# Shared slots for weights times values, transposes in 64-row tiles, and dummy matmuls at the start

## The chip, the cores and the metric

One core of one Trainium2 chip runs the kernel. The metric is the device time of one execution in microseconds; the median of three runs before is 609.94 us (609.64 to 611.61). The engines named are TensorE (PE; its weight loads stand apart as PEld), VectorE (DVE), ScalarE (ACT), GpSimd (POOL) and SyncE (SP, which issues most of the DMAs). Each works through its own queue in order; they wait for each other by semaphores.

## The reference

Attention with a threshold, then a gated feed-forward layer. Batch 8, 8 heads, sequence 576, head size 64; 4608 tokens of 512 go into the second part, whose hidden width is 1536.

```python
scores = scale * np.matmul(q, k.transpose(0, 1, 3, 2))
thresh = np.max(scores, axis=-1, keepdims=True) - tau
scores = np.where(scores >= thresh, scores, -1000000000.0)
attn = np.exp(scores - np.max(scores, axis=-1, keepdims=True))
attn = attn / (np.sum(attn, axis=-1, keepdims=True) + 1e-09)
x = np.matmul(attn, v)                    # heads side by side: 4608 x 512
xn = x / np.sqrt(np.mean(x * x, axis=-1, keepdims=True) + 1e-06) * rms_g
g = xn @ w_gate
out = (g * (1.0 / (1.0 + np.exp(-g))) * (xn @ w_val)) @ w_out
```

## The kernel before

**Tiling.** Queries go in chunks of 128: four "main" chunks for each batch (512 of the 576 rows), and for each two batches one "joined" chunk of their two tails of 64 rows. That makes 36 chunks. Heads go in pairs, four to a chunk, since the 64 channels of two heads fill 128 partitions. A chunk with a pair of heads is a step; there are 144, numbered s.

**A step.** `emit_s` issues the score burst, in float32: for either head (a half of the rows of the array) 512 columns and 64 tail columns, into `s_ps` (two tiles of two banks). These are matmuls of 64 rows; in a joined chunk they are 64 rows by 64 columns. VectorE passes over the scores of each head (line 441), which copies them to `ssb` and takes the maximum. GpSimd makes the threshold (448), ScalarE masks and exponentiates, or GpSimd masks (459 to 497). The weights `wsb` are transposed to `wt`: on TensorE in the first 16 steps (508 to 522), by DMA afterwards (525). `emit_av` multiplies with the values (544; in a joined chunk 549), ten matmuls of 128 rows (in a joined chunk twenty), into `ot`, one bank that two steps fill by halves. After every second step `emit_half` divides by the sums (570, 571), and the next matmuls into `ot` wait for it. After the fourth pair, `emit_x` normalizes the chunk and transposes it by DMA.

**The feed-forward part** (`emit_ffn`) works on groups of one to four chunks: for each of 12 blocks of the hidden width four matmuls for the gate (633) and four for the value (638), tanh on ScalarE (647), two passes on VectorE (650, 655); then 12 matmuls a chunk for the output (674).

**Inputs.** For each batch and pair `emit_qk` loads k and q (128 rows of 4 x 128) and transposes them on TensorE: four full 128 by 128 transposes for k, four for q (273), each four in a bank of their own, which VectorE or ScalarE copies to `qkT` (281, 283). The tails of k are transposed in 64-row tiles (304), those of q in full ones (321).

**Banks.** PSUM has eight banks: four for `s_ps`, one for `ot`, three in `ring`. From the ring come the banks of the feed-forward products, of all transposes of q and k, and of the first steps' transposed weights. After the last scores the four banks of `s_ps` join it.

**The order** is worked out in Python before the launch. Each piece of work is an `Op` with an engine, an estimated cost, a priority (mostly the step at which it is due), its dependencies, and how many ring banks it takes. `order_ops` plays the program through: of what an engine could do next it takes what can start first, and among equals what is due first. The instructions are issued to each engine in that order. A "gated" Op also depends on the score burst of a given step, so that a load isn't issued too early.

**Start.** The identity and constants are made, the first q and k are loaded, and TensorE starts with their transposes. The feed-forward weights are loaded and cast to float16 during the first steps (725 to 729). The cast of the gate weights is planned on VectorE and that of the value weights on GpSimd; the function that issues it reads `w_dram` when it is called, after the loop, so both are issued on GpSimd.

Of the kernel before, what the change touches and what calls it, by code (L numbers as in the profile page):

```python
# [15 lines left out]
COST = dict(  # L16
    s_main=1260.0, s_virt=1250.0, tr4=480.0, tr8=560.0, av_main=360.0, av_virt=500.0, ffn4=216.0,
    ttr=690.0, evac_qk=600.0, evac_kt=350.0, prelu=700.0, exp2=1250.0, exp1=690.0, exp0=690.0,
    mask_d=750.0, mask_g=1740.0, take_g=1300.0,
    trw=560.0, evac_w=420.0, rz=180.0, xmul=400.0, sq=800.0, xn=750.0, pool_tiny=270.0, pool_mean=800.0, pool_dma=800.0, cast_v=720.0, cast_vt=380.0, cast_w=720.0, sp=350.0, sp_tr=1300.0, sp_qk=1310.0, sp_tl=630.0,  # L20
)


class Op:
    __slots__ = ("eng", "cost", "prio", "deps", "fn", "ring", "frees", "slot", "end", "start", "dma", "opens", "nring")

    def __init__(self, eng, cost, prio, deps, fn, ring=None, frees=None, dma=0.0, nring=1):
# [5 lines left out]
        self.nring = nring  # L33


def order_ops(ops, ring_sizes):
# [17 lines left out]
    dma_free = 0.0  # L54
    out = []
    ready_at = {i: 0.0 for i in range(len(ops))}
    while len(out) < len(ops):
        best = None
        for e, lst in pending.items():
# [4 lines left out]
            for i in lst:  # L64
# [6 lines left out]
                k = (t, o.prio, i)  # L71
# [5 lines left out]
        o = ops[i]  # L77
        o.start = t
# [6 lines left out]
        eng_free[e] = t + o.cost  # L85
        if o.dma:
            dma_free = max(dma_free, t + 300.0) + o.dma
            o.end = max(dma_free, t + o.cost) + (1400.0 if o.cost == COST["sp_tr"] else 2000.0)
        else:
            o.end = t + o.cost  # L90
# [17 lines left out]
def kernel(  # L108
# [120 lines left out]
    def setup():  # L229
        o_id = add("POOL", 2000.0, -100, [], lambda o: make_identity(nc, id32))  # L230

        def consts(o):
            nc.vector.memset(zrow, 0.0)
# [9 lines left out]
        o_c = add("DVE", 400.0, -100, [o_id], consts)  # L243
# [8 lines left out]
    def emit_qk(b, p, prio):  # L252
# [16 lines left out]
        done = []  # L269
        for j in (1, 0):  # L270
            def tr(o, j=j):
                for c in range(4):
                    nc.tensor.transpose(ring[o.slot[0]][:, 128 * c:128 * c + 128],  # L273
                                        nat[:, j, c].rearrange("s h d -> s (h d)"), id32)

            t = add("PE", COST["tr4"], prio, [los[1 - j], o_id] + last_s.get(("k", b - 2, p), []), tr, ring="R")
# [550 lines left out]
```

## Time and profile before

| what | value |
|---|---|
| median of three runs | 609.94 us (609.64 to 611.61) |
| the profiled execution | 609.41 us |
| its span, first to last instruction | 607.3 us |
| mean granted TensorE clock | 0.999 |
| ScalarE: prelu pass (459), 224 times | 766 ns |
| weights transposed by DMA (525) | 128 times, median 3.0 us to landing |

The page gives each engine's busy time as a union of its instructions. TensorE's matmuls overlap, so their lengths are longer than the distance from one to the next; a group's true price on TensorE is read from its first start to the start of what follows. In a row of the timeline stand the start and the length of a run of equal instructions, the line, the shape and the count; "64*128" is the part of the array used, rows by columns. In a row of stretches stand its bounds and length, busy time and count of PE, PEld, DVE, ACT and POOL, then the clock, the DMA engines' busy share and GB/s.

### The profile page before, as it was taken

Reading aid. Unit: us, or ns where it says so; the run is one execution under the profiler, and the core shown is the slowest. Engines: PE = TensorE matmul, PEld = TensorE weight load, DVE = VectorE, ACT = ScalarE, POOL = GpSimd, SP = SyncE. Lnnn points to the kernel's source line nnn. Section 1 sums busy time; section 2 is a strip of 40 time slices with the busy share of each in tenths; the row PEclk is TensorE's granted clock in tenths of the full one; section 3 lists DMA queues with packets and bytes.
Section 4 is the critical chain, followed back from the end, with each engine's and each line's share of the span. In section 5 each row is a group of like instructions: output and inputs, shape, how many; then the busy total and the mean of one; then the engine's idle time right before and its main releaser. Section 6 shows DMA issues by size and latency. Waiting matters only on the chain.

```text
span 607.3 us, 13784 instructions
## 1 busy us (share of the span) xinstructions
PE 583.5 (96%) x5008; PEld 351.4 (58%) x5008; DVE 428.4 (71%) x1105; ACT 464.0 (76%) x741; POOL 322.2 (53%) x462
## 2 busy tenths in 40 slices
PE   5899899999999999999999999999999999999995
PEld 4676566767676555555555455555545445555663
DVE  3888775969686687748874887388747784887453
ACT  3898786878788888868886888688868886887332
POOL 0457774646475765654664557455565554653000
PEclk9999999999999999999999999999999999999999
DMA  9999797786786478677777467966779555435210
GB/s 180 251 238 225 146 166 180 161 159 122 181 166 157 108 146 165 157 179 131 173 167 167 103 132 175 189 140 148 141 177 168 105 89 126 119 87 101 65 37 35
DMA packets 271123, 88.99 MB, mean 147 GB/s; under 512 B 253648, under 2 KB 263376, under 8 KB 271056
## 3 DMA queue, kind: packets, MB, share of 16 engines
q1 hardware_dynamic: 268400, 86.28, 65.5%
q0 software_dynamic: 1600, 1.57, 1.7%
q8 instruction: 39, 0.64, 0.5%
q10 hardware_dynamic: 1056, 0.26, 0.2%
q14 instruction: 28, 0.23, 0.1%
HBM read 37.75 MB, written 9.44 MB: 78 GB/s over the span
## 4 chain that ended last, share of the span: by engine, by line
PE 69%; DMA 7%; issue 6%; ACT 6%; POOL 5%; DVE 5%; SPq 1%; DVEq 0%; POOLq 0%; ACTq 0%
PE s_ps L408 19%; PE ring L633 11%; PE ring L674 11%; PE ring L638 11%; DMA wt<-wsb 6%; PE ot L544 5%; PE ring L273 3%; PE s_ps L420 2%; ACT ssb L459 2%; DVE ssb L441 2%; POOL wsb L497 2%; POOL wsb L492 1%; PE s_ps L633 1%; DVE sl L650 1%; PE s_ps L638 1%
## 5 line engine op out<-in xcount | busy, mean ns | idle before, releaser
L441 DVE CUSTOM_DVE_ANT_0 ssb<-s_ps,zrow 128x576 f32<-128x576 f32 x288 | 208.8, 753 | 72.1 <-PE s_ps L408 62.2
L459 ACT ACTIVATE ssb<-ssb,nth 128x576 f32<-128x576 f32 x224 | 165.2, 766 | 39.4 <-POOL nth L448 38.9
L408 PE MATMUL s_ps<-qkT 64*128 64x512 f32 x512 | 156.6, 645 | 1.8 <-DVE mx L441 1.0
L448 POOL TENSOR_SCALAR nth<-mx 128x2 f32<-128x2 f32 x144 | 31.6, 220 | 158.3 <-DVE mx L441 147.3
L492 POOL TENSOR_SCALAR wsb<-ssb,nth 128x576 f16<-128x576 f32 x64 | 110.5, 1726 | 5.9
L638 PE MATMUL ring<-xnT,wv 128*128 128x512 f16 (+2 forms) x536 | 109.7, 327 | 1.4 <-DVE sl L650 1.2
L633 PE MATMUL ring<-xnT,wg 128*128 128x512 f16 (+2 forms) x536 | 109.3, 326 | 0.7 <-DVE wt L519 0.5
L466 ACT ACTIVATE wsb<-ssb 128x1152 f16<-128x1152 f32 x80 | 92.9, 1162 | 2.2
L674 PE MATMUL ring<-wo,hf 128*128 128x512 f16 x408 | 93.1, 379 | 0.0
L408 PEld LDWEIGHTS s_ps<-kTt,qkT 64*128 64x128 f32 x512 | 57.9, 188 | 55.8 <-issue 53.2
L650 DVE SCALAR_TENSOR_TENSOR sl<-th,ring 128x512 f32<-128x512 f32 (+2 forms) x134 | 73.5, 548 | 22.3 <-ACT th L647 21.6
L647 ACT ACTIVATE th<-ring 128x512 f32<-128x512 f32 (+2 forms) x134 | 64.2, 482 | 32.2 <-PE ring L633 31.5
L497 POOL TENSOR_TENSOR wsb<-wsb,esb 128x576 f16<-128x576 f16 x64 | 81.7, 1277 | 6.2 <-ACT esb L478 1.7
L655 DVE TENSOR_TENSOR hf<-ring,sl 128x512 f16<-128x512 f32 (+2 forms) x134 | 74.6, 557 | 8.6 <-PE s_ps L408 0.5
L633 PEld LDWEIGHTS <-wg 128*128 128x128 f16 x624 | 54.2, 98 | 33.3 <-issue 3.5
L638 PEld LDWEIGHTS <-wv 128*128 128x128 f16 x624 | 53.5, 98 | 32.6 <-issue 2.4
L674 PEld LDWEIGHTS <-hf 128*128 128x128 f16 x432 | 40.4, 98 | 46.5 <-issue 1.7
L544 PEld LDWEIGHTS <-wt 128*128 128x128 f16 x1280 | 52.2, 97 | 21.5 <-DMA wt<-wsb 7.5
L544 PE MATMUL ot<-va,wt 128*128 128x65 f16 x1280 | 60.0, 194 | 3.5 <-DMA wt<-wsb 3.3
L408 PEld LDWEIGHTS s_ps<-qkT 64*128 64x128 f32 x512 | 45.1, 185 | 30.7 <-issue 13.1
L478 ACT ACTIVATE esb<-ssb,nth 128x576 f16<-128x576 f32 x64 | 49.3, 770 | 10.6 <-POOL nth L448 10.3
L408 PE MATMUL s_ps<-kTt,qkT 64*128 64x64 f32 x512 | 49.9, 245 | 0.0
(54 smaller groups left out, 521.3 us busy)
## 6 DMA issues: line engine op xcount, KB each, us to landing
qkn<-in_k_dram SPq DMA_DIRECT2D x64, 128.0 KB, 3.1
vst<-in_v_dram SPq DMA_DIRECT2D x32, 256.0 KB, 3.2
out_dram<-osb SPq DMA_DIRECT2D x32, 256.0 KB, 2.7
qkn<-in_q_dram SPq DMA_DIRECT2D x62, 128.0 KB, 3.0
stage<-in_moe_w_gate_dram SPq DMA_DIRECT2D x12, 256.0 KB, 3.8
stage<-in_moe_w_val_dram SPq DMA_DIRECT2D x12, 256.0 KB, 4.0
wt<-wsb SPq DMA_TRANSPOSE x128, 3.0
wo<-in_moe_w_out_dram POOLq DMA_DIRECT2D x4, 384.0 KB, 8.0
```

The costliest lines, as they stand in the source:

```text
L408: nc.tensor.matmul(s_ps[h][:, at[h]:at[h] + n], qkT[b % 2][p][hs, c], src[hs], start=True, stop=True)
L441: nc.vector.tensor_tensor_reduce(out=ssb[a][:, h], in0=s_ps[h][:, ROW_AT[h]:ROW_AT[h] + S], in1=zrow, scale=-1.0 / 8.0, scalar=3.0e38, op0 ...
L459: nc.scalar.activation(out=ssb[a][:, h], in_=ssb[a][:, h], func=PRELU, scale=-1.0, bias=nth[m][:, h:h + 1], **PRELU_KW)
L466: nc.scalar.activation(out=wsb[s % NW], in_=ssb[a], func=AF.Exp)
L492: nc.gpsimd.tensor_scalar(out=wsb[s % NW][:, h], in0=ssb[a][:, h], scalar1=nth[m][:, h:h + 1], scalar2=None, op0=ALU.is_le)
L497: nc.gpsimd.tensor_tensor(out=wsb[s % NW][:, h], in0=wsb[s % NW][:, h], in1=esb[es], op=ALU.mult)
L544: nc.tensor.matmul(ot[:, cs], w[:, 4 * h + j], va[b % 2][:, p, V_AT[h][j]], start=(j == 0), stop=(j == 4))
L633: nc.tensor.matmul(ring[o.slot[0]][:, 0:n], wg[d][:, fs], xnT[slot][:, d, 0:n], start=(d == 0), stop=(d == 3))
L638: nc.tensor.matmul(ring[o.slot[0]][:, 0:n], wv[d][:, fs], xnT[slot][:, d, 0:n], start=(d == 0), stop=(d == 3))
L650: nc.vector.scalar_tensor_tensor(out=sl[i][:, 0:n], in0=th[i][:, 0:n], scalar=1.0, in1=ring[g.slot[0]][:, 0:n], op0=ALU.add, op1=ALU.mult)
L655: nc.vector.tensor_tensor(out=hf[hi][:, 0:n], in0=ring[vv.slot[0]][:, 0:n], in1=sl[i][:, 0:n], op=ALU.mult)
L674: nc.tensor.matmul(ring[o.slot[0]], hf[hs[fc][0]][:, 128 * j:128 * (j + 1)], wo[:, fc], start=(fc == 0), stop=(fc == NFC - 1))
```

## The change

1. **q and k in 64-row tiles.** From batch 1 on (`ROW_FROM`), `emit_qk` makes one Op of the transposes of k and q: sixteen transposes of 64 rows, alternating between the upper and the lower half of the rows, the upper into one ring bank and the lower into another. It takes both banks at once, waits for both loads, is gated by the score burst at its step, and has the priority -500, so that it comes first of what can start when that burst ends. The copies split by row half and write runs of 64 columns. The k tails get the same gate and priority; the q tails become eight 64-row transposes in two banks with two copies on ScalarE.
2. **Weights times values.** `ot` is gone; the ring has four banks. `emit_av` is called after every second step and issues both steps' matmuls (20, in a joined chunk 40) into one bank of the ring; reciprocal and product follow on VectorE as before and free the bank.
3. **Dummy matmuls.** `zrow` is cleared first, and eight matmuls of 512 columns of zeros into `s_ps` are the first work of TensorE.
4. **The order.** Estimated costs are new, and each Op of TensorE has a mode (full, 64-row, and the two of the joined chunks). A change of mode costs `SWITCH` = 170 ns in the plan. `BIAS`, which would let work of the same mode go first, is 0.
5. **Gate weights.** Their cast is planned on GpSimd, too.

`emit_s` is written in another way and issues the same matmuls in the same order; `N_ALT` equals `N_PE` and changes nothing.

```diff
+SWITCH = 170.0
...
-                k = (t, o.prio, i)
+                other = e == "PE" and o.mode != mode
+                k = (t + (BIAS if other else 0.0), o.prio, i)
...
+        cost = o.cost
+        if e == "PE":
+            if o.mode != mode:
+                t -= BIAS
+                cost += SWITCH
+            mode = o.mode
...
-    ot = ps("ot", 512)
-    ring = [ps(f"ring{i}", 512) for i in range(3)]
+    ring = [ps(f"ring{i}", 512) for i in range(4)]
...
+    HALF = (slice(0, 64), slice(64, 128))
...
+        o_z = add("DVE", 350.0, -200, [], lambda o: nc.vector.memset(zrow, 0.0))
+
+        def warm(o):
+
+            for _ in range(8):
+                nc.tensor.matmul(s_ps[0][:, 0:512], zrow[:, 0:128], zrow[:, 0:512], start=True, stop=True)
+
+        o_w = add("PE", COST["warm"], -200, [o_z], warm)
...
+        if b >= ROW_FROM:
+            def tr(o):
+                for j in (1, 0):
+                    for c in range(4):
+                        for r, rs in enumerate(HALF):
+                            at = 256 * j + 64 * c
+                            nc.tensor.transpose(ring[o.slot[r]][:, at:at + 64],
+                                                nat[rs, j, c].rearrange("s h d -> s (h d)"), id32[rs, rs])
+
+
+            t = gated(add("PE", COST["tr_qk"], -500.0, los + [o_id] + last_s.get(("k", b - 2, p), []), tr, ring="R",
+                          nring=2, mode=1), prio)
...
+                        nc.scalar.copy(out=dst[:, :, rs], in_=src)
...
+                        nc.vector.tensor_copy(out=dst[:, :, rs], in_=src)
...
-        t = add("PE", COST["tr4"], prio, [tail_load["k", b], o_id] + deps, tr, ring="R")
+        t = add("PE", COST["tr4"], prio if b < ROW_FROM else -500.0, [tail_load["k", b], o_id] + deps, tr, ring="R", mode=1)
+        if b >= ROW_FROM:
+            gated(t, prio)
...
             for p in range(NP):
-                nc.tensor.transpose(
-                    ring[o.slot[0]][:, 128 * p:128 * (p + 1)],
-                    qtl[i % 2][:, 2 * p:2 * p + 2].rearrange("s h d -> s (h d)"), id32)
+                for r, rs in enumerate(HALF):
+                    nc.tensor.transpose(
+                        ring[o.slot[r]][:, 64 * p:64 * (p + 1)],
+                        qtl[i % 2][rs, 2 * p:2 * p + 2].rearrange("s h d -> s (h d)"), id32[rs, rs])
...
+            for i in range(2):
+                w, p = wt[(s - 1 + i) % NWT], p1 - 1 + i
+                for h in range(2):
+                    at = (2 * i + h) * (D + 1)
+                    rows = [(slice(0, 128), b % 2)] if kind == "m" else [(HALF[e], e) for e in range(2)]
+                    for rs, vi in rows:
                         for j in range(5):
-                            nc.tensor.matmul(ot[64 * e:64 * e + 64, cs], w[:, 4 * h + j, 64 * e:64 * e + 64],
-                                             va[e][:, p, V_AT[h][j]], start=(j == 0), stop=(j == 4))
+                            nc.tensor.matmul(ring[o.slot[0]][rs, at:at + D + 1], w[:, 4 * h + j, rs],
+                                             va[vi][:, p, V_AT[h][j]], start=(j == 0), stop=(j == 4))
...
-        if s >= 2:
-            deps.append(half_ev[s // 2 - 1])
-        o = add("PE", COST["av_main" if kind == "m" else "av_virt"], s + 2.5, deps, fn)
+        deps = w_ready[s - 1] + w_ready[s] + [x for bb in bs for i in range(2) for x in v_ready[bb, p1 - i]]
+        o = add("PE", 2 * COST["av_main" if kind == "m" else "av_virt"], s + AV_PRIO, deps, fn, ring="R",
+                mode=0 if kind == "m" else 3)
...
-                    eng = nc.vector if w_dram is moe_w_gate else nc.gpsimd
-                    eng.tensor_scalar(
+                    nc.gpsimd.tensor_scalar(
...
-        emit_av(s)
         if p % 2:
-            emit_half(s)
+            emit_av(s)
...
-    seq = order_ops(ops, {"R": 3})
+    seq = order_ops(ops, {"R": 4})
```

More of the change, by code (lines that the diff above doesn't have):

```diff
@@ L89, in order_ops @@
         else:
-            o.end = t + o.cost
+            o.end = t + cost
         if o.frees is not None:
@@ L570, in fn, with half @@
+        o = add("PE", 2 * COST["av_main" if kind == "m" else "av_virt"], s + AV_PRIO, deps, fn, ring="R",
+                mode=0 if kind == "m" else 3)
+        for i in range(2):
+            av_of[s - i] = [o]
+            for bb in bs:
+                last_av[bb, p1 - i] = last_av.get((bb, p1 - i), []) + [o]
+        r = rz[len(half_ev) % 3]
+        def half(_):
+            o3 = ring[o.slot[0]][:, 0:4 * (D + 1)].rearrange("p (h d) -> p h d", d=D + 1)
             nc.vector.reciprocal(out=r, in_=o3[:, :, D])
@@ L733 @@
                 lo = gated(add("SP", COST["sp"], pr, w_use[slot][-1:], load, dma=1050.0), pr)
-                ca = (add("DVE", 420.0, pr, [lo, o_g], cast) if w_dram is moe_w_gate
-                      else add("POOL", COST["cast_w"], pr, [lo, o_g], cast))
+                ca = add("POOL", COST["cast_w"], pr, [lo, o_g], cast)
                 w_use[slot].append(ca)
@@ L781 @@
 ON_ACT = 1
+BIAS = 0.0
+ROW_FROM = 1
+AV_PRIO = 2.5
+HALF_PRIO = 1.2
 WAYS = ("pg", "pp")
```

130 lines of the change are left out of this document (59 added, 71 removed).

## The prediction

> **What bounds the kernel now.** I read the head of the page first, then the busy time by stretch, then the chain that ended last.
>
> ```profile
> span 607.3 us, 13784 instructions
> PE 583.5 (96%) x5008; PEld 351.4 (58%) x5008; DVE 428.4 (71%) x1105; ACT 464.0 (76%) x741; POOL 322.2 (53%) x462
> 30.00:60.00 30.00, 29.71 (x300) 21.51 (x297) 25.71 (x73) 27.66 (x40) 20.13 (x39) 1.00 0.98 231
> 60.00:90.00 30.00, 27.56 (x318) 18.09 (x315) 23.14 (x67) 23.55 (x40) 22.14 (x30) 1.00 0.89 157
> 90.00:570.00 480.00, 474.55 (x3934) 274.31 (x3934) 343.07 (x856) 383.39 (x604) 272.52 (x373) 1.00 0.68 145
> PE 69%; DMA 7%; issue 6%; ACT 6%; POOL 5%; DVE 5%; SPq 1%; DVEq 0%; POOLq 0%; ACTq 0%
> ```
>
> From 90 to 570 us TensorE is busy 474.55 of 480 us, while ScalarE has 383, VectorE 343 and GpSimd 273. The DMA engines stand at 0.68. There, a microsecond of TensorE work saved is close to a microsecond of time. From 30 to 60 us ScalarE (27.66 of 30) and VectorE (25.71) are as full as TensorE, so I count nothing for TensorE work saved before 90 us. The chain agrees: 69% of it is TensorE.
>
> A busy TensorE is not one at its best rate, so I take costs from start to start in the timeline of TensorE. (Its columns: start, length, instruction, shape, count.)
>
> ```profile
> 150.63 1.13 PE L408 MATMUL s_ps<-qkT 64*128 64x512 f32 x4
> 151.60 0.33 PE L408 MATMUL s_ps<-kTt,qkT 64*128 64x64 f32 x4
> 151.86 0.61 PE L638 MATMUL ring<-xnT,wv 128*128 128x256 f16 x4
> ...
> 153.19 0.47 PE L544 MATMUL ot<-va,wt 128*128 128x65 f16 x10
> 153.49 0.63 PE L273 MATMUL ring<-id,qkn 128*128 128x128 f32 x4
> 153.96 0.47 PE L544 MATMUL ot<-va,wt 128*128 128x65 f16 x10
> 154.36 1.13 PE L408 MATMUL s_ps<-qkT 64*128 64x512 f32 x4
> ```
>
> A score burst holds TensorE 1.23 us (150.63 to 151.86). Ten weights-times-values matmuls take 0.30 us when a transpose follows (153.19 to 153.49) but 0.40 when a score burst follows (153.96 to 154.36). So entering the 64-row form costs 0.10 us. Leaving it: from the four small score matmuls at 151.60, two a half, to the next form are 0.26 us; two steps of 0.06 (as of the tails' transposes below, which are of the same form) are work, so some 0.15 us is the way out. Transposes and weights-times-values, both 128 by 128, follow each other without such a price.
>
> **Part 1: q and k transposed in 64-row tiles.** The old price of a batch and head pair is two groups of four 128-row transposes.
>
> ```profile
> 34.06 0.66 PE L273 MATMUL ring<-id,qkn 128*128 128x128 f32 x4
> 34.55 0.47 PE L544 MATMUL ot<-va,wt 128*128 128x65 f16 x10
> ...
> 92.07 1.07 PE L273 MATMUL ring<-id,qkn 128*128 128x128 f32 x8
> 92.97 1.89 PE L674 MATMUL ring<-wo,hf 128*128 128x512 f16 x8
> ...
> 90.00:570.00 480.00, 28.41 (x192) 21.26 (x192) 1.00 0.68 145
> ```
>
> Four cost 0.47 to 0.49 us, eight in a row 0.90. I take 0.92 for a pair of head's q and k. The last row is line 273 alone: 192 transposes between 90 and 570 us, that is 24 pairs. The other eight pairs lie before 90 us; four of them (batch 0) aren't changed anyway.
>
> The new form is 16 transposes, alternating between the two halves of the rows, into two banks. The trace has none of these, but it has the tail's transposes, which already are 64-row tiles of one half:
>
> ```profile
> 162.06 0.69 PE L408 MATMUL s_ps<-qkT 64*128 64x512 f32 x1
> 162.16 0.35 PE L304 MATMUL ring<-id,ktl 64*128 64x64 f32 x3
> L304 PE MATMUL ring<-id,ktl x4: 222/223/272, 162.0 to 162.3; 64*128 64x64 f32 x4
> ```
>
> Three span 0.35 us and one lasts 0.223, so each starts 0.06 us after the one before. They run while a score matmul of the other row half streams (162.06 to 162.75): the two halves go side by side. So 16 transposes in two halves are eight steps of 0.062, 0.50 us, if both halves are fed; one after the other they would be 1.0 us. These are my two ends, and I take 0.50, because the rows above show the halves running at once. Behind a score burst they pay no entry, and the way out only moves behind them. Saved: 0.92 - 0.50 = 0.42 us, times 24 = **10.1 us**. Where other work slips between burst and transposes, 0.10 + 0.15 comes on top. For that, two of four banks must be free at the burst's end; during its 1.23 us nothing takes a bank, so I let one in seven miss: 24/7 x 0.25 = **-0.9 us**.
>
> ```profile
> L304 PEld LDWEIGHTS ring<-id,ktl x4: 136/138/139, 162.0 to 162.2; 64*128 64x128 f32 x4
> L273 PEld LDWEIGHTS ring<-id,qkn x192: 137/141/145, 92.0 to 462.3; 128*128 128x128 f32 x192
> ```
>
> A weight load of 64 rows takes 138 ns, one of 128 rows 141. [...]
>
> The tails follow the same way.
>
> ```profile
> 429.57 0.46 PE L304 MATMUL ring<-id,ktl 64*128 64x64 f32 x4
> 429.96 1.04 PE L633 MATMUL ring<-xnT,wg 128*128 128x512 f16 x4
> 90.00:570.00 480.00, 2.75 (x24) 1.93 (x24) 1.00 0.68 145
> ...
> 490.41 0.57 PE L549 MATMUL ot<-va,wt 128*64 128x65 f16 x20
> 490.90 1.10 PE L420 MATMUL s_ps<-qkT,qTv 64*64 64x512 f32 x8
> ```
>
> A k tail between other forms costs 0.39 us plus 0.10 entry; behind a burst 4 x 0.06 = 0.24: 0.25 saved. Of the six after 90 us (24 instructions, third row, line 304 alone) the one at 162 us already sat at a burst, so 5 x 0.25 = **1.3 us**. The q tails, four full transposes at 0.49 as above, become four double steps of 0.25: three after 90 us, **0.7 us**.
>
> ScalarE and VectorE copy the same 512 columns per pair as before, in another order; each q tail becomes two ScalarE copies, off the path. The transposes now wait for both the k and the q load, which are issued three of the 144 steps (3 x 607/144 = 12.6 us) ahead.
>
> **Part 2: two pairs' weights-times-values together.** Twenty matmuls instead of ten are the same work. In the chunks of joined tails they are a form of their own (128*64): the burst at 490.41 takes 0.49 us and entry and exit are in each. Twelve of the sixteen lie after 90 us and become six: 6 x 0.2 = **1.2 us**. The waits:
>
> ```profile
> PE ot L544 <- DMA wt<-wsb: 3.3, 6, 0.9
> PEld L544 <- DMA wt<-wsb: 7.5, 11, 1.4
> ```
>
> TensorE stood between 3.3 us (matmuls) and 7.5 us (weight loads) for late transposed weights. One wait for two pairs lets the earlier of them be late for free; nothing to all of it could go, and I take **2 us**. What waits behind it in TensorE's queue is everything, which is why a late pair would now cost the same but be met half as often. The bank of `ot` joins the ring: three banks become four, and one is held per two steps. New waits for banks in an order that is worked out afresh are not in the trace; between -3 and +4 us, I take **-1.5 us**.
>
> **Part 3: dummy matmuls.**
>
> ```profile
> L273 PE MATMUL ring<-id,qkn x8: 421/421/446, 5.9 to 7.5; 128*128 128x128 f32 x8
> L273 PE MATMUL ring<-id,qkn x192: 272/273/330, 92.1 to 462.4; 128*128 128x128 f32 x192
> 5.94 1.94 PE L273 MATMUL ring<-id,qkn 128*128 128x128 f32 x8 [5.94 <-DMA qkn<-in_k_dram]
> 8.75 2.08 PE L408 MATMUL s_ps<-qkT 64*128 64x512 f32 x4 [0.26 <-DVE qkT L283]
> 11.09 2.12 PE L273 MATMUL ring<-id,qkn 128*128 128x128 f32 x12
> ```
>
> The clock column doesn't show it, but the durations do: the first transposes last 421 ns against 273 later, and the first score burst (8.75 to 11.09) takes 2.34 us against 1.23. The array starts at about half speed until some 12 us. Eight dummies of 512 columns, 0.43 us each at that speed, fill about 1.4 to 4.9 us, when TensorE waits for the first load anyway. If the clock then stays up, the first transposes and scores shrink by 0.9 + 1.1 us; if it doesn't, nothing. From 30 us on ScalarE is nearly full, and its work would start as much earlier. I take **1.5 us** of 0 to 2.
>
> That the clock falls back during the transposes from 5.94 us, so that the 1.5 us are 0, I give 0.3; the first score burst was still slow right after two microseconds of transposes. [...]
>
> **Part 4: gate weights.** The diff moves their cast from VectorE to GpSimd, but it was there:
>
> ```profile
> L729 POOL TENSOR_SCALAR wg<-stage,rmsg 128x512 f16<-128x512 f32 x12 | 8.3, 694 | 0.6
> ```
>
> The old lambda read a loop variable late. Only the order changes, before 90 us: 0.
>
> **Sum.** 10.1 - 0.9 + 1.3 + 0.7 + 1.2 + 2 - 1.5 + 1.5 = 14.4 us. The profiled execution took 609.41 us, 2.1 over its span, and lies 0.5 below the median of 609.94; span 592.9, time 595.0 against its own, 595.5 against the median: I say **595**.
>
> **The rivals.**
>
> A, *transposes away from the bursts.* If the banks are usually taken at a burst's end, other work goes first and every pair pays entry and exit: 24 x 0.25 = 6 us less than Part 1 counts, of which 0.9 is deducted already: 600. Against it: nothing takes a bank during a burst. Chance 0.12.
>
> B, *the halves do not run side by side.* Then 16 x 0.062 = 1.0 us replaces 0.92, Part 1's main term is -2 instead of 10.1, and the time is 607. For it: no row shows two transposes at once. Against it: the score matmul at 162.06 beside the tail's transposes. Chance 0.08. [...]
>
> C, *banks starve TensorE: slower.* The price comes from what holds the banks.
>
> ```profile
> L441 DVE CUSTOM_DVE_ANT_0 ssb<-s_ps,zrow 128x576 f32<-128x576 f32 x288 | 208.8, 753 | 72.1 <-PE s_ps L408 62.2
> L283 DVE COPY qkT<-ring 128x512 f32<-128x512 f32 x32 | 22.0, 688 | 22.5 <-PE ring L273 19.3 <-ACT ssb L459 2.8 <-ACT osb L680 0.3
> L647 ACT ACTIVATE th<-ring 128x512 f32<-128x512 f32 (+2 forms) x134 | 64.2, 482 | 32.2 <-PE ring L633 31.5
> L650 DVE SCALAR_TENSOR_TENSOR sl<-th,ring 128x512 f32<-128x512 f32 (+2 forms) x134 | 73.5, 548 | 22.3 <-ACT th L647 21.6
> ```
>
> Right behind a burst VectorE has two score passes (753 ns each) ahead of its copy (688): one bank is held 2.2 us from the burst's end, ScalarE's half up to 1.5 us, and a pair's weights-times-values may hold a third. The feed-forward then has one bank, and after each product must wait for 482 + 548 ns of reading, 1.0 us of idle TensorE per pair of head. It decides from 14.4 / 24 = 0.6 us per pair; at 1.0 the time is 609.4 - 14.4 + 24 = 619. Against it: at 92.07 eight transposes took two of three banks, and TensorE went on at 92.97, in the 0.90 us that eight at 0.11 need. Chance 0.06.
>
> **How the numbers follow.** Forecast 0.72, A 0.12, B 0.08, C 0.06, and 0.02 for no effect at all. D, *the clock falls back* (0.3, whatever the other case), moves a time by 1.5 us: 596.5 in the forecast, inside its bounds. The forecast's own bounds: everything in Part 1 behind bursts (+0.9), the wait term up to 5 more, banks +5 to -2, clock -1.5 to +0.5; together, not all at once, 588.5 to 601. A lies inside; reaching out toward B, the range is 588.5 to 603.5 and leaves out B, C and the rest, 0.16. A measurement here can tell about 0.3%, 1.8 us: forecast, A and most of B are faster (0.91), 0.03 the same, 0.06 slower.
>
> **What would show it.** Line 273's successor in 64*128 form, 16 matmuls spanning about 0.5 us plus a tail, directly behind line 408's rows: right; 1.0 us: B. Feed-forward or weights-times-values between them: A. TensorE idle on `sl` or `hf` beside them, more than in the page above: C. The first transposes at 273 ns: Part 3 right; 421: wrong. TensorE's idle for `wt` under 3 us: Part 2 right. Wrong in any case if, from 90 to 570 us, the busy time falls but the stretch does not shorten.

## The result, and the profile after

The changed kernel takes 595.03 us (median of four runs, 593.09 to 597.22), the kernel before on the same chip 610.29 (609.64 to 611.61). The ratio is 0.9748 with the interval 0.9703 to 0.9793: faster by 2.5%. The profiled execution of after took 597.22 us with a span of 595.1; the profiled one of before took 609.41 with 607.3.

The head of the page of after, its chain by engine, and then its view of stretches (bounds and length; busy time and count of PE, PEld, DVE, ACT, POOL; clock; DMA share; GB/s):

```profile
span 595.1 us, 14293 instructions
PE 577.8 (97%) x5256; PEld 344.3 (58%) x5256; DVE 424.9 (71%) x1105; ACT 462.9 (78%) x745; POOL 322.4 (54%) x462
PE 80%; DVE 6%; DMA 5%; ACT 4%; POOL 3%; issue 2%; SPq 1%; DVEq 0%; POOLq 0%
90.00:570.00 480.00, 475.02 (x4209) 273.22 (x4210) 347.41 (x873) 383.37 (x616) 271.38 (x369) 1.00 0.70 145
```

TensorE is still the bound, and its share of the chain rose from 69 to 80%. In the 480 us it stays as busy as before but issues 4209 matmuls instead of 3934; 176 of these 275 come of the transposes of q and k alone, which are smaller and more (368 instead of 192). So a busy share can't tell what was gained; the steps can. VectorE passes over each step's scores twice (line 483 of after); the start of the first of these passes marks the step. The table is worked out from these starts, one profiled execution each:

| us | before | after |
|---|---|---|
| start to step 48 | 186.1 | 186.7 |
| step 48 to step 143 | 366.7 | 354.7 |
| step 143 to the end | 54.5 | 53.7 |

Nearly all of the gain of these two executions, 12.0 of 12.2 us, lies in the middle. (The profiled execution of after is the slowest of its four; the medians differ by 15.3 us.)

The timeline of after, TensorE alone, at the places that were named beforehand:

```profile
94.30 0.71 PE L293 MATMUL ring<-id,qkn 64*128 64x64 f32 x16
94.94 0.61 PE L668 MATMUL ring<-xnT,wg 128*128 128x256 f16 x4
...
320.73 1.13 PE L463 MATMUL s_ps<-qkT 64*128 64x512 f32 x4
...
321.86 0.67 PE L293 MATMUL ring<-id,qkn 64*128 64x64 f32 x16
322.46 2.76 PE L709 MATMUL ring<-wo,hf 128*128 128x512 f16 x12
...
427.03 1.13 PE L463 MATMUL s_ps<-qkT 64*128 64x512 f32 x4
...
428.16 0.41 PE L345 MATMUL ring<-id,ktl 64*128 64x64 f32 x4
428.50 1.04 PE L673 MATMUL ring<-xnT,wv 128*128 128x512 f16 x4
```

A burst with sixteen transposes behind it holds TensorE 1.73 us (320.73 to 322.46), 0.50 more than the 1.23 of a burst alone; one with a k tail 1.47 (427.03 to 428.50), 0.24 more. Of the 28 pairs of head changed, 24 stand right behind a burst, 21 of the 23 after 90 us; the one at 94.30 stands alone and holds 0.64 (94.30 to 94.94) beside its entry.

TensorE's waits over the whole span, two rows of before (the bursts of main and of joined chunks stand in two lines there, in one line of after) and then, in the second fence, three of after (in all, times, the longest):

```profile
PEld s_ps L408 <- DVE mx L441: 9.5, 21, 1.2
...
PEld s_ps L420 <- DVE mx L441: 3.9, 10, 0.6
```

```profile
PEld s_ps L463 <- DVE mx L483: 25.0, 63, 1.0
PEld L589 <- DMA wt<-wsb: 2.0, 4, 0.9
PE ring L589 <- DMA wt<-wsb: 1.5, 3, 0.8
```

The waits for late transposed weights went from 3.3 us (matmuls) and 7.5 (weight loads) to 1.5 and 2.0. Another wait grew beside them: the weight loads of score bursts come up to VectorE, which still reads the scores before (`mx`), 63 times and for 25.0 us instead of 31 times and 13.4 us. A weight load that waits doesn't stop the matmuls that still run: the matmuls themselves waited 4.1 us for `mx` in after, 1.8 in before.

### The profile page after: what moved, and what is told of

The parts are those of the page before. It is cut to its first block, busy times and chain, and to the rows that moved or that the text cites. A ratio compares the mean times of both kernels' runs of the same rounds, so it can differ in the third digit from the quotient of the medians.

```text
span 595.1 us, 14293 instructions
## 1 busy us (share of the span) xinstructions
PE 577.8 (97%) x5256; PEld 344.3 (58%) x5256; DVE 424.9 (71%) x1105; ACT 462.9 (78%) x745; POOL 322.4 (54%) x462
## 4 chain that ended last, share of the span: by engine, by line
PE 80%; DVE 6%; DMA 5%; ACT 4%; POOL 3%; issue 2%; SPq 1%; DVEq 0%; POOLq 0%
PE s_ps L463 28%; PE ring L709 13%; PE ring L668 13%; PE ring L673 12%; PE ring L589 6%; DVE ssb L483 3%; DMA wt<-wsb 3%; PE ring L293 2%; ACT ssb L501 2%; PE s_ps L709 1%; PE s_ps L673 1%; PE ring L553 1%; PE s_ps L668 1%; DMA qkn<-in_q_dram 1%; ACT wsb L508 1%
## 5 line engine op out<-in xcount | busy, mean ns | idle before, releaser
L463 PE MATMUL s_ps<-qkT 64*128 64x512 f32 x512 | 162.9, 645 | 4.7 <-DVE mx L483 3.2
L668 PE MATMUL ring<-xnT,wg 128*128 128x512 f16 (+2 forms) x548 | 111.0, 325 | 0.4 <-DVE xsb L606 0.3
L463 PEld LDWEIGHTS s_ps<-kTt,qkT 64*128 64x128 f32 x512 | 61.0, 188 | 54.0 <-issue 51.3
L709 PE MATMUL ring<-wo,hf 128*128 128x512 f16 x396 | 89.9, 379 | 0.0
L463 PEld LDWEIGHTS s_ps<-qkT 64*128 64x128 f32 x512 | 48.9, 185 | 45.8 <-DVE mx L483 21.9
L673 PEld LDWEIGHTS <-wv 128*128 128x128 f16 x624 | 55.4, 98 | 34.2 <-issue 1.6
L668 PEld LDWEIGHTS <-wg 128*128 128x128 f16 x624 | 52.5, 98 | 30.9 <-issue 1.0
L589 PEld LDWEIGHTS <-wt 128*128 128x128 f16 (+1 forms) x1600 | 52.2, 100 | 12.4 <-issue 2.3
L589 PE MATMUL ring<-va,wt 128*128 128x65 f16 (+1 forms) x1560 | 56.4, 194 | 1.7 <-DMA wt<-wsb 1.5
L463 PE MATMUL s_ps<-kTt,qkT 64*128 64x64 f32 x512 | 54.3, 245 | 0.0
```

The source lines that it names most:

```text
L463: nc.tensor.matmul(s_ps[h][rows, at[h]:at[h] + n], lhs(hs), src[hs], start=True, stop=True)
L589: nc.tensor.matmul(ring[o.slot[0]][rs, at:at + D + 1], w[:, 4 * h + j, rs], va[vi][:, p, V_AT[h][j]], start=(j == 0), stop=(j == 4))
L668: nc.tensor.matmul(ring[o.slot[0]][:, 0:n], wg[d][:, fs], xnT[slot][:, d, 0:n], start=(d == 0), stop=(d == 3))
L673: nc.tensor.matmul(ring[o.slot[0]][:, 0:n], wv[d][:, fs], xnT[slot][:, d, 0:n], start=(d == 0), stop=(d == 3))
L709: nc.tensor.matmul(ring[o.slot[0]], hf[hs[fc][0]][:, 128 * j:128 * (j + 1)], wo[:, fc], start=(fc == 0), stop=(fc == NFC - 1))
```

## The experiments

The kernels differ from after as their diffs show; e9 differs from before. Each runs beside before on its chip, and only the ratios are compared from one chip to another. The order is worked out anew for every edit that changes an Op, so a difference holds the edit and its order together. Two kernels keep the order exactly: e4 is after itself, and e8 changes the order inside one Op alone.

**After again (e4).** No edit; the mark against which the others stand.

> The changed kernel once more, on the same chip as its parts: 595 us by its four runs (593.1 to 597.2). It gives the spread that the others are held against; if the dummies release the clock in some executions, the times fall into two groups about 2 us apart.

Measured: 598.39 us, ratio 0.9772 (0.9741 to 0.9803); span 593.7. Steps 48 to 143 took 353.1 us against 354.7 in the first profile of after: a difference under 2 us between two single profiles says nothing. The five times lie in two groups, 595.6 to 595.9 and 598.4 to 598.8, as expected for dummies that release the clock in some executions. But the profiled one is of the lower group, and its clock rose only at 13.27 us; so the dummies don't explain its group, and what does is open.

**Full transposes for q and k (e1).**

```diff
-ROW_FROM = 1
+ROW_FROM = 8
```

> The changed kernel with q and k of all batches transposed in full 128-row tiles again (the tails stay in 64-row tiles). If the transposes are what pays, as the prediction has it (10.1 - 0.9 us), this takes 9 us more than the changed kernel, some 604 us, and line 314 has 256 full transposes with nothing of line 293. If the new order and the fourth bank pay instead, it stays within 2 us of the changed kernel, some 596.

Measured: 603.67 us, 0.9877 (0.9841 to 0.9912), span 601.1. The 64-row form is worth 5.3 us by the medians, where Part 1 counted 9.2 for these pairs. What else the change does gains 7.8 us without it (611.5 before on this chip). e1's row of the weight loads that wait for `mx`, over the whole span, is nearly that of after:

```profile
PEld s_ps L463 <- DVE mx L483: 23.7, 59, 1.1
```

**The transposes half by half (e8).** The same sixteen, all of the upper row half first. Nothing else moves.

```diff
-                for j in (1, 0):
-                    for c in range(4):
-                        for r, rs in enumerate(HALF):
+                for r, rs in enumerate(HALF):
+                    for j in (1, 0):
+                        for c in range(4):
```

> The changed kernel with the sixteen transposes in another order: all eight of the upper row half, then all eight of the lower. If the halves run side by side only because neighbours in the queue alternate, the sixteen take 1.0 us instead of 0.5 and the time rises by 24 x 0.5 = 12 us, to 610. If each half has a queue of its own, the burst stays at 0.5 us and the time within 2 us of the changed kernel.

Measured: 597.7 us, 0.9792 (0.9765 to 0.982), span 596.1. The timeline of e8 at the same burst as above, and the stretch 90 to 570 us of the transposes alone (PE, PEld) of e8:

```profile
321.88 1.13 PE L463 MATMUL s_ps<-qkT 64*128 64x512 f32 x4
...
323.01 0.96 PE L293 MATMUL ring<-id,qkn 64*128 64x64 f32 x16
323.91 1.25 PE L709 MATMUL ring<-wo,hf 128*128 128x512 f16 x5
...
90.00:570.00 480.00, 22.93 (x371) 21.90 (x369) 1.00 0.72 145
```

The transposes now hold 0.90 us (323.01 to 323.91) where after has 0.60 (321.86 to 322.46), and are busy 22.93 us between 90 and 570 us (16.98 in after). So the halves do run side by side, and less so in e8's order than in the alternating one. And the price came out far below what such a microsecond should cost. In distances from one start to the next, summed over the span, the transposes took 25.2 us instead of 19.6, 5.6 more; score bursts took 171.1 instead of 173.3. So 2.2 of the 5.6 came back, and all of it in the 32 bursts that follow the transposes of a pair (44.6 us instead of 46.8, in e4 also 46.8; the other bursts differ by 0.1 at most). I read this as a burst that starts later and finds VectorE done; the waits don't show it, for e8's weight loads of bursts stand for `mx` 63 times and 24.9 us, as in after. Weights times values fell as well, from 44.5 to 42.9, but in e4, the same kernel as after, they took 42.7. Both kernels are, within their intervals, equally fast.

This also bears on e1. There q and k take 34.7 us of TensorE in this sum, in e8 33.3 and in after 27.4, the first four pairs included. These four took 6.5 us in e1, where the clock had risen in time, and 8.1 in e8, so for the other 28 pairs it is 28.2 against 25.2. Yet e8 is faster than e1 by 0.85% of before, 5 us. So part of what the 64-row form gains over e1 isn't TensorE's time in the transposes; its place behind a burst and the order around it are what is left, and no run separates these.

**One pair's weights times values at a time, in a bank of its own (e2).** This undoes Part 2: `ot` is back, the ring has three banks.

```diff
-    ring = [ps(f"ring{i}", 512) for i in range(4)]
+    ot = ps("ot", 512)
+    ring = [ps(f"ring{i}", 512) for i in range(3)]
...
-        if p % 2:
-            emit_av(s)
+        emit_av(s)
+        if p % 2:
+            emit_half(s)
...
-    seq = order_ops(ops, {"R": 4})
+    seq = order_ops(ops, {"R": 3})
```

> The changed kernel with the weights times values of one pair at a time in their own bank, and three ring banks, as before. By the prediction (1.2 + 2 - 1.5 us) it takes 1 to 3 us more than the changed kernel, 597. If the shared slot and the fourth bank are the real gain, 6 us more or above, over 601. If the row transposes starve on three banks, more than that, with TensorE idle for sl and hf.

Measured: 618.43 us, 1.0111 (1.0072 to 1.015), span 616.1: 20 us behind e4 and slower than before. e2's waits of TensorE over the whole span, and of the stretch 372 to 448 us one of GpSimd; then its timeline (TensorE, and one row of SyncE's queue):

```profile
PE ot L587 <- DMA wt<-wsb: 7.2, 9, 2.1
PEld L587 <- DMA wt<-wsb: 12.9, 13, 2.2
...
POOL nth L491 <- DVE mx L484: 26.5, 7, 14.4
```

```profile
420.56 1.30 SPq L283 DMA_DIRECT2D qkn<-in_q_dram  x2
...
422.04 1.45 PE L464 MATMUL s_ps<-qkT 64*128 64x512 f32 x4
...
437.32 1.03 PE L682 MATMUL ring<-xnT,wv 128*128 128x512 f16 x4
438.28 0.27 PE L294 MATMUL ring<-id,qkn 64*128 64x64 f32 x1
438.89 0.71 PE L294 MATMUL ring<-id,qkn 64*128 64x64 f32 x15 [0.34 <-DVE sl L694]
439.69 2.75 PE L718 MATMUL ring<-wo,hf 128*128 128x512 f16 x12
442.37 1.13 PE L464 MATMUL s_ps<-qkT 64*128 64x512 f32 x4
```

Two losses can be seen. Late weights cost 7.2 and 12.9 us, as in before and more. And there is one hole: no score burst starts between 422.04 and 442.37, and GpSimd waits 14.4 us for a maximum. TensorE is mostly busy there, with feed-forward work. The next burst needs q and k, whose loads were issued at 420.56 and earlier and land 3.3 us later (the median of this stretch); their transposes stand at 438.28, behind the whole feed-forward group, and wait there for a bank that the feed-forward part held (`sl`). `order_ops` shows why such an Op comes late:

```python
if len(ring_free[o.ring]) < o.nring:
    continue
t = max(t, sorted(ring_free[o.ring])[o.nring - 1][0])
```

An Op for two banks is no candidate, or a late one, while the feed-forward part takes each single bank as it comes free; its priority of -500 decides only between equal starts. This reading is of the rows and the code; an order that keeps banks back for such an Op wasn't tried.

**Neither (e5).** e2 with `ROW_FROM = 8`; dummies, tails and estimated costs stay as in after.

> The changed kernel with both undone: full transposes for q and k, and one pair's weights times values at a time in its own bank with three ring banks; new costs, tails in 64-row tiles and dummies stay. If the two parts simply add up (5 us for the transposes, 20 for the shared slot, as the first four runs gave them one by one), it takes 623 us. If instead the 64-row transposes need the fourth bank, so that the loss of the second run is theirs, it is near the kernel before: 608 to 612.

Measured: 617.97 us, 1.0145 (1.0122 to 1.0168), span 614.9. That should have been near before and is 1.5% slower. The steps place it: 367.3 us from step 48 to 143, as before (366.7), but step 16, the first joined chunk, starts at 73.7 us instead of 63.2. The timeline of e5 there:

```profile
49.39 0.66 SPq L336 DMA_DIRECT2D qtl<-in_q_dram  x1
...
62.86 1.01 PE L682 MATMUL ring<-xnT,wv 128*128 128x256 f16 x4 [1.95 <-DVE sl L694]
...
70.61 0.27 PE L366 MATMUL ring<-id,qtl 64*128 64x64 f32 x1
71.17 0.46 PE L366 MATMUL ring<-id,qtl 64*128 64x64 f32 x7 [0.29 <-DVE sl L694]
...
72.35 1.10 PE L464 MATMUL s_ps<-qkT,qTv 64*64 64x512 f32 x8
```

It looks like the same hole: the q tail, issued at 49.39 and landed 8.4 us later, is transposed only at 70.61; in its new form it, too, asks for two of three banks. That form needn't open a hole, though: in e2 and e6, with the same form and as many banks, this tail is transposed at 60.46 and 61.86. The clock fell there as well, for 3.4 us from 62.28 on, in TensorE's wait of 1.95 us (60.91 to 62.86).

**Two pairs together, but in a bank of their own (e6).** Ring of three.

```diff
-nc.tensor.matmul(ring[o.slot[0]][rs, at:at + D + 1], w[:, 4 * h + j, rs],
+nc.tensor.matmul(ot[rs, at:at + D + 1], w[:, 4 * h + j, rs],
...
-    seq = order_ops(ops, {"R": 4})
+    seq = order_ops(ops, {"R": 3})
```

> The changed kernel, two pairs' weights times values still issued together, but into a bank of their own, with three ring banks. If the missing fourth bank is what cost 20 us in the second run, this is as slow, 615 us or more, with TensorE waiting for sl, hf and mx. If issuing two pairs together is what pays, it stays within 3 us of the changed kernel, 598 to 601.

Measured: 605.69 us, 0.9927 (0.9904 to 0.9949), span 604.4. Against after's steps it loses 6.0 us in the middle (360.7) and 3.5 at the end (57.2). The waits for late weights stay away, the fourth bank is what is missing (with one bank, each two pairs also wait until VectorE has read the two before); e6's row of TensorE's waits for them, over the whole span:

```profile
PE ot L590 <- DMA wt<-wsb: 1.2, 3, 0.8
```

**A shared slot, but each pair as soon as its weights are there (e7).** Ring of four; the first pair takes the slot, the second fills it.

```diff
+            slot = (first or o).slot[0]
...
-        deps = w_ready[s - 1] + w_ready[s] + [x for bb in bs for i in range(2) for x in v_ready[bb, p1 - i]]
+        deps = w_ready[s] + [x for bb in bs for x in v_ready[bb, p]] + [first]
...
+                ring=None if p % 2 else "R", mode=0 if kind == "m" else 3)
```

> The changed kernel with four ring banks, two pairs sharing a slot, but the first pair's matmuls issued as soon as its weights are there, not together with the second's. If the fourth bank pays, it stays within 2 us of the changed kernel, 598 to 600. If waiting once for two pairs pays, it is near the second run, over 610, with TensorE idle for wt as there (6.6 us) or more.

Measured: 615.34 us, 1.0084 (1.0055 to 1.0113), span 613.6. Here the bank is there and the pairing is missing. e7's waits, and a row of its timeline ahead of step 16:

```profile
PE ring L590 <- DMA wt<-wsb: 3.3, 8, 0.8
PEld L590 <- DMA wt<-wsb: 8.0, 13, 1.1
...
65.57 1.01 PE L676 MATMUL ring<-xnT,wv 128*128 128x256 f16 x4 [3.08 <-DVE sl L688]
```

The waits for weights are back at the size of before (3.3 and 8.0 us). The slot is also held for longer, from the first pair to after the second, and the hole ahead of the first joined chunk is back as well (step 16 at 72.6 us). From step 48 to 143 it took 366.0 us.

**The 64-row pairs alone, in the kernel before (e9).** Only q and k; tails, three banks, `ot` and costs as before.

```diff
+        if b >= ROW_FROM:
...
+            t = gated(add("PE", COST["tr_qk"], -500.0, los + [o_id] + last_s.get(("k", b - 2, p), []), tr, ring="R",
+                          nring=2), prio)
...
+ROW_FROM = 1
```

> The kernel before with nothing but the sixteen 64-row transposes for q and k (from batch 1 on, behind a burst, in two of its three banks); costs, tails, weights times values and start as before. If TensorE's work sets the time in any order, it gains what 28 pairs save, 9 to 11 us, and takes 599 to 601. If two of three banks starve TensorE (the rival on the slower side), it is slower than before, over 612, with waits for sl, hf and mx. In between, about 606, if both are true.

Measured: 614.64 us, 1.0063 (1.0037 to 1.0088), span 613.0. Alone, the part that carried 9.2 of my 14.4 us makes the old kernel slower by 4 us. e9's waits of TensorE:

```profile
PE ot L568 <- DMA wt<-wsb: 4.8, 11, 1.0
PE ot L573 <- DMA wt<-wsb: 3.0, 3, 1.8
PEld s_ps L432 <- DVE mx L465: 20.0, 47, 0.9
PEld s_ps L444 <- DVE mx L465: 4.8, 10, 0.9
```

TensorE got the pairs done for less, 28.7 us instead of 35.5 in distances of starts over the span. But score bursts took 198.7 instead of 192.8 in the same sum, weights times values 57.0 instead of 53.7 and the products for the gate 104.1 instead of 100.1 (those for the value 102.4 instead of 104.2). The waits fit: the weight loads of bursts stood 24.8 us for `mx` against 13.4 in before, the matmuls 7.8 us for late weights (two rows) against 3.3.

**The old costs (e10).** The cost table of before and no price for a change of mode; all else as in after.

```diff
-SWITCH = 170.0
+SWITCH = 0.0
```

> The changed kernel with the estimated costs of the kernel before and no price for a change of mode in the plan. If the order only has to be about right, because pairs and four banks leave slack, it stays within 3 us of the changed kernel, 595 to 600. If the new costs carry part of the gain, it is 604 or more; if they cost something, as the slow run with both parts undone (618) may mean, it is under 594.

Measured: 596.72 us, 0.9776 (0.9743 to 0.9809), span 595.0: the same as after. The new estimates bring nothing.

**No dummies (e3), and twelve of them (e11, e12).**

```diff
-        o_w = add("PE", COST["warm"], -200, [o_z], warm)
```

> The changed kernel without the eight dummy matmuls. In the profile of the changed kernel the first transposes still take 421 ns, so the dummies gave nothing: the time stays within 1 us of the changed kernel. If the dummies do release the clock in most executions, and only the profiled one missed it, this is 1.5 to 2 us slower.

Measured for e3: 598.30 us, 0.9783 (0.9755 to 0.9811), span 596.2, against 598.39 with the eight dummies on the same chip. For e11 `COST["warm"]` became 5100, too; e12 adds `SLACK = 150`, a margin in the plan for what TensorE waits for.

```diff
-            for _ in range(8):
+            for _ in range(12):
```

> The changed kernel with twelve dummies instead of eight. The clock rose early only where its 3.4 us window was filled by about three quarters or more with dummies; twelve, 5.1 us, do that wherever the windows lie. Then the first transposes take 273 ns in every execution, step 8 starts about 1.3 us earlier and the time is 1 to 2 us under the changed kernel, 594 to 597 here. If dummies do not decide it, the first transposes stay at 421 ns and it is equal or, for the later first transposes, up to 0.5 us slower.

> Twelve dummies, and the plan lets TensorE's work wait 150 ns longer for what it needs from another engine (SLACK = 150). In the changed kernel TensorE reaches score bursts before VectorE has left the scores (its weight loads waited 25 us for mx, 9.5 before). If these waits are lost time, other work takes their place and this is 2 to 5 us under the run with twelve dummies alone. If they only lie beside running matmuls, it is equal to it within 1 us, or a little slower.

Measured: e11 591.61 us (591.51 to 592.64), 0.9699 (0.9672 to 0.9725), span 589.4; e12 593.68, 0.9734 (0.9705 to 0.9763), span 591.7. **e11 is the fastest version of this study**, 5.1 us below e10 on the same chip. The margin of e12 was to show whether the waits for `mx` are lost time; it left them almost as they were (57 times and 23.8 us, 60 and 25.5 in e11), so it doesn't tell. The first matmuls of after:

```profile
1.22 3.60 PE L247 MATMUL s_ps<-zrow 128*128 128x512 f16 x8 [1.22 <-DVE zrow L242]
6.06 1.94 PE L314 MATMUL ring<-id,qkn 128*128 128x128 f32 x8 [1.25 <-DMA qkn<-in_k_dram]
8.88 2.08 PE L463 MATMUL s_ps<-qkT 64*128 64x512 f32 x4 [0.26 <-DVE qkT L324]
...
L314 PE MATMUL ring<-id,qkn x8: 418/418/445, 6.1 to 7.6; 128*128 128x128 f32 x8
```

And of e11:

```profile
1.21 4.51 PE L247 MATMUL s_ps<-zrow 128*128 128x512 f16 x12 [1.21 <-DVE zrow L242]
5.99 1.06 PE L314 MATMUL ring<-id,qkn 128*128 128x128 f32 x8 [0.27 <-DMA qkn<-in_k_dram]
7.93 1.13 PE L463 MATMUL s_ps<-qkT 64*128 64x512 f32 x4 [0.49 <-ACT kTt L356]
...
L314 PE MATMUL ring<-id,qkn x8: 272/273/299, 6.0 to 6.8; 128*128 128x128 f32 x8
```

With eight dummies the first transposes still last 418 ns; with twelve they last 273, and the first score burst 1.13 us instead of 2.08. How much of e11's gain this is, is less plain, because its order was worked out anew as well. Step 8 starts 1.8 us earlier than in after, step 48 2.2 us, the end 5.7; the 12.7 us between steps 34 and 35 of after, also without a hole in TensorE's work, are not in e11. So some 2 us belong to the start, and the rest wasn't separated.

**All in one table.** Where each kernel's steps lie, as worked out above:

| us | start to step 16 | start to step 48 | 48 to 143 | 143 to end |
|---|---|---|---|---|
| before | 63.2 | 186.1 | 366.7 | 54.5 |
| after | 61.3 | 186.7 | 354.7 | 53.7 |
| e1, full q and k | 66.8 | 187.6 | 359.7 | 53.8 |
| e8, half by half | 61.4 | 187.2 | 355.1 | 53.7 |
| e6, three banks, pairs together | 65.6 | 186.5 | 360.7 | 57.2 |
| e7, four banks, one pair at a time | 72.6 | 193.9 | 366.0 | 53.7 |
| e2, three banks, one pair at a time | 64.3 | 189.1 | 377.9 | 49.0 |
| e5, e2 with full q and k | 73.7 | 193.4 | 367.3 | 54.3 |
| e9, before with 64-row q and k | 64.5 | 186.7 | 374.4 | 51.9 |
| e11, twelve dummies | 58.3 | 184.5 | 351.2 | 53.7 |
| e12, twelve and a margin | 57.0 | 182.5 | 358.7 | 50.5 |

Read in the middle column, the two main parts depend on each other. With full transposes, Part 2 is worth 7.6 us (367.3 to 359.7), with 64-row ones 23.2 (377.9 to 354.7), most of it the hole in e2. The 64-row form gains 5.0 us where Part 2 is there (359.7 to 354.7) and loses 10.6 where it isn't (367.3 to 377.9). But the columns trade with one another: feed-forward work that one order does in the middle, another does later (e2 and e12 end sooner), and the hole of e5 lies ahead of this column. By the ratios of the whole time Part 2 is worth 2.7% with full transposes (e5 to e1) and 3.4% with 64-row ones (e2 to e4); the 64-row form gains 1.1% where Part 2 is there (e1 to e4), and where it isn't, e2 and e5 differ by no more than their intervals. That it can lose by itself is shown by e9.

## Why the prediction was right, and which of its steps were not

The time was right, 595 predicted and 595.03 measured, and so was the place: at step 48 (186 us) after is still 0.5 us behind, and all is gained between there and the end. But the sum came out by errors that cancel, and that it came out so close is luck: on the chip of e4 the same two kernels differ by 13.1 us, here by 15.3, and 14.4 were counted.

- **Part 1, the price of sixteen transposes: right.** 0.50 us behind a burst, 21 of 23 pairs after 90 us placed so; one in seven was to miss, two did. Rival A (away from the bursts) is out.
- **Part 1, its worth: wrong.** The step was "a microsecond of TensorE work saved is close to a microsecond of time". e8 gives 5.6 us of TensorE back and loses 0.2% by the ratios against e4 (0.8% between the outer ends of the two intervals), 0.4% against the first runs of after; e1 shows 5.3 us for the pairs where 9.2 were counted. Where the rest went is shown in part. In e8 the bursts behind the transposes give 2.2 of 5.6 us back, which I read as waiting that they did in after. In distances of starts, q and k take 7.3 us less in after than in e1 (27.4 against 34.7), but all score bursts 1.1 more (194.5 against 193.4), though they should take 2.4 less by my 0.10 for the change of form, which has moved behind 24 pairs: an estimate of 3.5 us that the bursts took back. The count of waits for VectorE's maximum doesn't show this, for it is nearly as high in e1 (59 and 63, and 31 in before); most of its rise belongs to the other parts of the change. I read from a busy share of 99% that nothing else could come next; the waits for `mx` stood in the waits view of before with 13.4 us, and I didn't price them.
- **Rival B, halves one after the other.** Such a price was seen, 0.90 us in e8, but there it costs some 1 to 3 us (0.2 to 0.4%) and not the 12 that I gave it: 0.30 us more a pair instead of 0.50, of which the bursts took part back. The length of a single weight load doesn't decide it: one of the new form takes 139 ns in after (median), so sixteen one after the other would be 2.2 us, but a pair's sixteen pass in 0.64 us (321.75 to 322.39), so they overlap.
- **The tails.** A k tail behind a burst costs 0.24 us as counted. Of the three q tails after 90 us one gains what was counted in after (0.35 us behind a burst, from 329.95 on, 0.25 more than the burst alone); behind the one at 195.70 the next burst waits for VectorE, and the one at 464.54 stands behind weights times values. Their two-bank form stands in the hole of e5, but e2 and e6 have the form without the hole, and e7, with four banks, has the hole too (69.14).
- **Part 2: right in kind, mis-sized.** The terms for waits and banks, 2 and -1.5, were nearly nothing together. By e1, all that isn't q and k gains 7.8 us; e10 and e3 show no gain from costs and dummies, so with the tails' 1 us or so (an estimate) Part 2 is near 6 to 7 where 1.7 was predicted (against e5, which is slower than before, it is 16). The waits for weights fell under 3 us, as named beforehand, but more was at stake than the 3.3 to 7.5 us of that row: against e4, e7 loses 3.1% of before's time with those waits back and its slot held longer, and e6, without the fourth bank, 1.6%.
- **Rival C, banks: present, in another form.** I argued against it that nothing takes a bank during a burst. e2 and e9 are that rival's kernels, and they are slower than before (1.0111 and 1.0063). But the feed-forward part didn't wait for the transposes' banks, as C says. In e2 the transposes, which need two banks at once, came behind the feed-forward part, and the score bursts with them. With the fourth bank and the pairing, no such hole is left in after from step 48 on: no two steps in a row start more than 7.9 us apart, in e2 19.6. How much of e9's loss is of that kind wasn't settled: it has no single hole above 10 us, but more waits for weights and for `mx`.
- **Part 3: wrong.** 1.5 us were counted, none measured: the eight dummies took 3.60 us in after (0.45 each, 0.43 was an estimate), and the first transposes last 418 ns. Rival D named another cause, a clock that rises and falls back; in after it didn't rise in time at all (first at 12.52 us), in e5 it did what D says (up at 4.26 us, down at 7.67). Transposes didn't keep the clock down in e10: it rose at 13.79 us, at the end of 3.41 us of which they held 2.9 (10.69 to 13.60). With twelve dummies the first transposes lasted 273 ns (median) in both profiles.
- **The gate weights and costs: nothing, right** (e10).

In sum after 90 us 12.9 us were predicted and, from step 48 to the end, 12.8 measured in the two profiled executions; Part 1 brought about four fewer and Part 2 about five more. With the two parts so bound to each other no single split is exact.

## What to carry to other kernels

Before a saved microsecond is counted as time, look in the waits view for the engine that the bounding one meets next, even if it meets it only 31 times; changing only the order inside one piece of work, so that the plan stays as it is, shows cheaply what a microsecond there is worth. In a plan that takes what can start first, work that needs two buffers at once can be starved by work that needs one, whatever its priority, so more buffers or fewer, larger takers can be worth more than the faster instruction. Compare waits by what waits, not by line number: here one line of after stands for two of before. Judge the parts of a change in both company and isolation: here the 64-row form is a gain in the whole change and a loss in the kernel before.

## What the runs showed of the hardware that was not expected

**Alternating row halves.** Sixteen 64-row transposes add 0.50 us to a burst when the queue alternates the halves, and 0.80 (321.88 to 323.91, less 1.23) in two blocks of eight. So the two halves overlapped less when eight of one half stood together in the queue.

**The clock changed at distances of 3.41 us, and it fell after a stretch in which TensorE was busy for 58%.** Eight dummies raised the clock in time (first transposes at 273 ns, not 418) in two of nine profiled executions (e1 and e5), twelve in both of theirs. In e5 it then fell back; e5's stretches with PE's busy time first and the clock as third number from the end:

```profile
4.30:7.60 3.30, 1.75 (x14) 1.18 (x12) 0.56 (x1) 0.76 (x2) 0.00 (x0) 1.00 1.27 210
7.70:11.00 3.30, 3.12 (x12) 2.07 (x13) 0.75 (x4) 0.10 (x1) 0.00 (x0) 0.50 1.00 195
```

After has the same in its middle, where before has none:

```profile
196.80:200.20 3.40, 1.97 (x8) 1.15 (x9) 2.06 (x7) 3.37 (x8) 2.83 (x5) 1.00 0.11 23
200.30:203.60 3.30, 3.30 (x18) 1.66 (x19) 0.87 (x3) 3.24 (x5) 2.55 (x4) 0.50 0.48 107
203.70:207.10 3.40, 3.40 (x44) 1.77 (x43) 1.52 (x5) 2.33 (x5) 2.20 (x3) 1.00 0.76 171
```

After a stretch with TensorE busy for 1.97 of 3.40 us, the next has the clock at 0.50: the joined burst that starts at 200.23 us holds TensorE 2.73 us, the one at 205.12 only 1.14. So a stall of 1.4 us was followed by 3.41 us at 0.50 (200.25 to 203.66). The busy share alone doesn't decide it. In e2 a stretch of the same length, which begins 70 times 3.413 us after that kernel's first rise, was less full (1.79 of 3.40 us), and the clock stayed up (its mean over the span is 0.999); e2's stretch:

```profile
256.30:259.70 3.40, 1.79 (x19) 1.04 (x18) 1.96 (x4) 2.05 (x5) 2.71 (x4) 1.00 1.36 102
```

What decides there is open. Within one execution the changes lie whole multiples of the same length apart: in e5 the records of the clock change at 4.26, 7.67 and 11.08 us, 3.41 apart, and in after the first rise (12.52 us) and the fall (200.25) are 55 times 3.413 us apart. From one execution to the next the place differs: the first rise of kernels with the same eight dummies lies anywhere from 4.26 (e5) to 17.33 us (e2). My reading, which no run tests by itself, is that this is why eight dummies of 3.6 us reach it in some executions only, and 4.5 to 5.3 us of them in both: the 3.41 us that ended with the rise were filled by dummies to 82% in e1 and 89% in e5, while a stretch filled to 74% in after (2.28 to 5.69 us, counted back from its rise) brought none. But the next stretch of after (5.69 to 9.10 us), in which TensorE was busy for 2.78 us with transposes and scores, brought none either. Two executions with twelve are few to rely on.
